# The first projection of a two-layer transformer kernel: two token tiles only centred ahead of q, their deviation applied to the logits

## Chip, cores, metric

The kernel runs on one core of a Trainium2 chip. The metric is the device time of one execution in microseconds (us), the median over several executions. "The block" below is the long run of 512-column matmuls that makes up 98% of the time. Its start is read from the timeline (start of its first matmul); the chain of waits, which counts from the end of the work before it, puts the same point up to 0.2 us later.

## The reference, cut to what matters

```python
x = A_x                                            # 2048 tokens x 1024, bf16
x = x + _A_ref(_layernorm(x), A_wqkv, A_wo)        # attention over 8 tokens at distance 0, 2, .. 14
x = x + _B_ref(_layernorm(x), B_w1, B_w3, B_w2)    # gated feed-forward, 1024 -> 3584 -> 1024
x = x + _A_ref(_layernorm(x), A_wqkv, A_wo)        # the same two once more, same weights
x = x + _B_ref(_layernorm(x), B_w1, B_w3, B_w2)

def _layernorm(x, axis=-1, eps=1e-5):
    m = jnp.mean(x, axis=axis, keepdims=True)
    v = jnp.var(x, axis=axis, keepdims=True)
    return (x - m) / jnp.sqrt(v + eps)
```

q, k and v are the normalised x times 1024 x 1024 weights. Since the layer norm divides each token by its own deviation, q of a token can be computed from the centred x, and its logits multiplied by 1/deviation afterwards.

## The kernel before

The kernel builds a list of operations, places them with a small scheduling model and emits them in that order; each engine then follows its own fixed order. All DMA is issued by one queue (SyncE), strictly in order. Token tiles have 128 tokens, chunks 512. The start works on chunk 0:

```python
def q_first():
    load_x(0, 0, 2)                      # token tiles 0, 1
    wslots[0] = q_weights(0, "k")        # eight rows of q weights, 256 KB each
    load_x(0, 2, 4)                      # tiles 2, 3
    b = ln(0, first=True)                # per tile: bn_stats x2, bn_aggr, sqrt (ScalarE), reciprocal,
                                         # (x - mean) * rstd, 8 TensorE transposes, copy to xnT
    order = [(0, 0, 5), (1, 0, 5), (0, 5, 8), (1, 5, 8), (2, 0, 8), (3, 0, 8)]
    for j, k0, k1 in order:              # tile by tile: matmuls of 128 columns
        ...
                    nc.tensor.matmul(bank[...][:, (m % 4) * P:(m % 4 + 1) * P], lhsT=lk[m][0],
                                     rhs=xnT[b][:, kk, j * P:(j + 1) * P], ...)
    ...                                  # store q, load k weights, x of chunk 1, v weights ...
    for which, key, tile_ in ((1, "kT", kT), (2, "vT", vT)):
        q_tile(0, 0, which, wslots[which], b, (key, tile_))   # k and v: 512-column matmuls, the block begins
```

Of the kernel before, what the change touches and what calls it, by code (L numbers as in the profile page):

```python
# [154 lines left out]
def kernel(  # L155
# [24 lines left out]
    scale = float(Dh) ** -0.5  # L180
    EPS = 1e-5
    NSLOT = 6
    NWARM = 12

    xin = A_x[0].rearrange("(n p) d -> p n d", p=P)
    xout = out[0].rearrange("(n p) d -> p n d", p=P)
# [11 lines left out]
    def alloc(name, shape, dt=BF16):  # L198
        return sb.tile(shape, dt, name=name)
# [29 lines left out]
    rs = alloc("rs", [P, NE], FP32)  # L229
    rsb = alloc("rsb", [P, NE])  # L230
    An = alloc("An", [P, W, NE])
    oT = [alloc(f"oT{i}", [P, KT, TCH]) for i in range(2)]
    qkv_d = [[dram.tile([D, S], BF16, name=f"qkv_d{l}_{i}") for i in range(3)] for l in range(2)]
    bank = [pp.tile([P, 512], FP32, name=f"bank{i}") for i in range(8)]
# [6 lines left out]
    def t1(n):  # L241
        return 0.15 + n / 960.0

    def dve(dur, emit, reads, writes, cls=2, **kw):
        return pr.add("DVE", dur, emit, reads, writes, cls, **kw)
# [4 lines left out]
    def dma(kb, dst, src, reads, writes, cls=3, transpose=False):  # L250
        def emit(op):
            if transpose:
                nc.sync.dma_start_transpose(dst, src)
            else:
                nc.sync.dma_start(dst, src)  # L255
        return pr.add("SP", 0.45, emit, reads, writes, cls, size=kb * 1024)
# [28 lines left out]
    def take_slot():  # L285
        i = n_slot[0] % NSLOT
        n_slot[0] += 1
        return i

    def load_x(c, j0=0, j1=TPC, after=()):  # L290
        for j in range(j0, j1):
            n = c * TPC + j
            dma(256, x_sb[n][:], xin[:, n, :], after, [("x", n, 0), ("x", n, 1)], 0 if c == 0 else 3)
# [3 lines left out]
    def ln(c, first=False):  # L297
        s = stage_no[0]
        b, q = s % 2, s % 4
        xb = xnT[b]  # L300

        def stats(j):
            n = c * TPC + j
            pri = j - 9 if first else 1
            for hh in range(2):
                dve(0.67, lambda _, hh=hh: nc.vector.bn_stats(st[q][:, j, hh, :],  # L306
                                                              x_sb[n][:, hh * 512:(hh + 1) * 512]),
                    [("x", n, hh)], [("st", q, j, hh)], pri)
            dve(0.2, lambda _: nc.vector.bn_aggr(mv[q][:, j, :], st[q][:, j, :, :]),  # L309
                [("st", q, j, 0), ("st", q, j, 1)], [("mv", q, j)], pri)  # L310

        def root(j0, j1):
            act(0.3, lambda _: nc.scalar.activation(sd[q][:, j0:j1], mv[q][:, j0:j1, 1], ACTF.Sqrt, bias=epst[:]),  # L313
                [("mv", q, j) for j in range(j0, j1)] + ["eps"], [("sd", q, j) for j in range(j0, j1)], j0 - 9 if first else 0, table="sqrt")
            dve(0.16, lambda _: nc.vector.reciprocal(rstd[q][:, j0:j1], sd[q][:, j0:j1]),  # L315
                [("sd", q, j) for j in range(j0, j1)], [("rstd", q, j) for j in range(j0, j1)], j0 - 9 if first else 0)

        def apply(j):
            n = c * TPC + j
            dve(0.5, lambda _: nc.vector.tensor_scalar(xn[j][:], x_sb[n][:], mv[q][:, j, 0:1], rstd[q][:, j:j + 1],  # L320
                                                       op0=ALU.subtract, op1=ALU.mult),
                [("x", n, 0), ("x", n, 1), ("mv", q, j), ("rstd", q, j)], [("xn", j)], j - 9 if first else 1)

        if first:
            for j in range(TPC):
                stats(j)
                root(j, j + 1)
                apply(j)
                a = Acc()

                def tr(op, j=j, a=a):
                    pt = bank[a.bank][:].bitcast(BF16)
                    for kk in range(KT):
                        nc.tensor.transpose(pt[:, kk * P:(kk + 1) * P], xn[j][:, kk * P:(kk + 1) * P], ident[:])  # L334
                tro = pr.add("PE", 0.5, tr, [("xn", j), "ident"], [], takes=[a], lag=0.17, lane=2)

                def ev(op, j=j, a=a):
                    pt = bank[a.bank][:].bitcast(BF16)
                    nc.scalar.copy(xb[:, :, j * P:(j + 1) * P], pt.rearrange("p (k t) -> p k t", k=KT))
                evac(act, 1.0, ev, tro, [], [("xnT", b, j)], a)  # L340
            return b
        for j in range(TPC):
            stats(j)
        root(0, TPC)
        for j in range(TPC):
            apply(j)
            dma(256, xb[:, :, j * P:(j + 1) * P], xn[j][:], [("xn", j)], [("xnT", b, j)], 0, transpose=True)
        return b
# [10 lines left out]
    def evac(add, dur, emit, last_mm, reads, writes, a, cls=0, **kw):  # L359
        op = add(dur, emit, reads, writes, cls, gives=[a], **kw)  # L360
        op.deps.add(last_mm)
        return op

    wslots = {}

    def q_weights(which, split):
        ids = [take_slot(), take_slot()]
        for h, i in enumerate(ids):
            if split != "c":
                v = slot[i][:].rearrange("p (k c) -> p k c", k=4)  # L370
                for k in range(0, 4, 1 if split == "k" else 4):
                    n = 1 if split == "k" else 4
                    dma(256 * n, v[:, k:k + n, :], wqkv_v[:, 4 * h + k:4 * h + k + n, which * D:(which + 1) * D], [],
                        [("w", i, k + z) for z in range(n)], 0 if split == "k" else 3)
            else:
                v = slot[i][:].rearrange("p (k c) -> p k c", k=KT)
                dma(1024, v, wqkv_v[:, :, which * D + h * 512:which * D + (h + 1) * 512], [],
                    [("w", i, k) for k in range(4)], 3)
        return ids, split
# [35 lines left out]
    def q_stage(l, c):  # L415
# [3 lines left out]
            q_tile(l, c, which, ws, b)  # L419
        stage_no[0] += 1  # L420

    def q_first():
        load_x(0, 0, 2)
        wslots[0] = q_weights(0, "k")
        load_x(0, 2, 4)
        b = ln(0, first=True)
        accs = {}
        order = [(0, 0, 5), (1, 0, 5), (0, 5, 8), (1, 5, 8), (2, 0, 8), (3, 0, 8)]
        for j, k0, k1 in order:
            if j not in accs:  # L430
                accs[j] = [Acc(), Acc()]
            pa = accs[j]
            for kk in range(k0, k1):
                lk = [q_lhs(wslots[0], kk, m) for m in range(KT)]

                def emit(op, kk=kk, j=j, pa=pa, lk=lk):
                    for m in range(KT):
                        nc.tensor.matmul(bank[pa[m // 4].bank][:, (m % 4) * P:(m % 4 + 1) * P], lhsT=lk[m][0],  # L438
                                         rhs=xnT[b][:, kk, j * P:(j + 1) * P], start=(kk == 0 and m % 4 == 0),
                                         stop=(kk == KT - 1), skip_group_check=True)  # L440
                op = pr.add("PE", 8 * 0.056, emit, [lk[0][1], ("xnT", b, j)], [], takes=pa, lag=0.17)
            if k1 == KT:
                for g in range(2):
                    evac(act, 0.59, lambda _, a=pa[g], g=g, j=j: nc.scalar.copy(
                        hT[:, 4 * g:4 * g + 4, j * P:(j + 1) * P],
                        bank[a.bank][:].rearrange("p (m t) -> p m t", m=4)), op, [],
                        [("hT", 4 * g + m, j) for m in range(4)], pa[g])
        for m0 in range(0, KT, 2):
            dma(256, spill_view(0, 0, m0, 0), hT[:, m0:m0 + 2, :],
                [("hT", m, j) for m in (m0, m0 + 1) for j in range(TPC)], [("d", 0, 0, 0, m0)], 1)  # L450
        wslots[1] = q_weights(1, "s")
        load_x(1)
        load_x(2, 0, 2)
        wslots[2] = q_weights(2, "s")
        load_x(2, 2, 4, [("hT", 7, TPC - 1)])
        load_x(3, 0, 4, [("hT", 7, TPC - 1)])
        for which, key, tile_ in ((1, "kT", kT), (2, "vT", vT)):
            dve(0.11, lambda _, tile_=tile_: nc.vector.memset(tile_[:, :, 0:HALO], 0.0), [], [(key, "h")], 1)
            q_tile(0, 0, which, wslots[which], b, (key, tile_))
        dma(2048, wo[:], wo_v, [("d", 0, 2, 0, 6)], ["wo"], 3)  # L460
        stage_no[0] += 1
# [25 lines left out]
    def t_stage(l, half):  # L487
# [22 lines left out]
                                                psm[:].rearrange("p w s -> p (w s)")), allA, ["pB"])  # L510
        dve(1.22, vtt(l2, psmT[:, :, 0:2], psmT[:, :, 2:4], ALU.add), ["pB"], [l2k])
        dve(t1(512), vtt(L.rearrange("p w e -> p (w e)"), l2[:, :, 0], l2[:, :, 1], ALU.add), [l2k], [Lk])
        if tok0 == 0:
            dve(t1(64), vtt(L[:, :, 0:8], L[:, :, 0:8], maskT[:], ALU.add), [Lk, "mask"], [Lk])
        dve(t1(256), vtt(m4, L[:, 0:4, :], L[:, 4:8, :], ALU.max), [Lk], [Lk])
# [157 lines left out]
```

## Time and profile before

| | before |
|---|---|
| time | 1617.48 us, 3 runs, 1617.37 to 1617.6 (later, with more runs, 1617.47) |
| span of the profiled run | 1615.7 us |
| first q matmul | 8.50 us |
| start of the block | 24.11 us |
| length of the block | 1588.69 us for 7416 matmuls, 214 ns each |

The chain of waits of the kernel before (start, length, what; all in us) shows the whole kernel in its last lines:

```profile
16.24 0.45 PE bank L334 x8
16.68 7.59 PE bank L438 x136
24.28 1588.69 PE bank L355 x7416
1612.97 0.02 issue
1612.99 0.29 DVE x L600
```

From 24.28 us on nothing delays TensorE. The table of who waited for whom, for TensorE (total us, times, longest), has only the start:

```profile
PE bank L334 <- DVE xn L320: 1.3, 2, 1.1
PE bank L278 <- DVE warm L274: 1.2, 1, 1.2
PE bank L438 <- ACT xnT L339: 0.4, 1, 0.4
```

L278 are the twelve warm-up matmuls, L334 the transposes, L438 the q matmuls. So an early change can only move the start of the block, as long as it leaves the block alone.

### The profile page before, as it was taken

How to read it: one execution, taken by the hardware profiler on the slowest of the kernel's cores; microseconds unless marked ns; L12 is line 12 of the kernel's file. 1: busy time of each engine (PE TensorE's matmuls, PEld its weight loads, DVE VectorE, ACT ScalarE, POOL GpSimd, SP SyncE). 2: the span in 40 equal slices, each digit the busy share in tenths (PEclk: the TensorE clock that was granted, in tenths of full speed). 3: DMA queues.
4: the chain of work that ended last, by engine and by line, in shares of the span. 5: the costliest groups of instructions: out<-in, count | busy, mean ns of one | idle time of the engine just before them, and what ended most of it. 6: DMA issues, size and time to landing. Idle time of an engine off the chain costs nothing.

```text
span 1615.7 us, 19394 instructions
## 1 busy us (share of the span) xinstructions
PE 1610.0 (100%) x7716; PEld 764.4 (47%) x7716; DVE 1120.2 (69%) x1900; ACT 328.9 (20%) x519; POOL 1.9 (0%) x12
## 2 busy tenths in 40 slices
PE   9999999999999999999999999999999999999999
PEld 7555544444444444444444444444444444444444
DVE  5898888889889888888898728884298832211211
ACT  4423322021211222113211032110321101101110
POOL 0000000000000000000000000000000000000000
PEclk9999999999999999999999999999999999999999
DMA  9734755385548763858545487465873464454441
GB/s 311 218 106 139 235 170 157 121 226 177 171 130 242 201 198 123 219 165 251 175 141 157 163 244 224 128 168 179 247 229 118 155 184 156 144 175 151 156 165 44
DMA packets 347818, 285.30 MB, mean 177 GB/s; under 512 B 70096, under 2 KB 342480, under 8 KB 347600
## 3 DMA queue, kind: packets, MB, share of 16 engines
q1 hardware_dynamic: 347728, 284.07, 57.9%
q8 instruction: 60, 0.98, 0.2%
q14 instruction: 30, 0.25, 0.0%
HBM read 238.94 MB, written 29.36 MB: 166 GB/s over the span
## 4 chain that ended last, share of the span: by engine, by line
PE 99%; DMA 1%; DVE 0%; SPq 0%; issue 0%
PE bank L355 98%; PE bank L438 0%; DMA x<-in_A_x_dram 0%; DMA slot<-in_A_wqkv_dram 0%; DVE st L306 0%; PE bank L334 0%; SPq L255 0%; DVE xn L320 0%; DVE mv L309 0%; DVE x L600 0%; DVE rstd L315 0%
## 5 line engine op out<-in xcount | busy, mean ns | idle before, releaser
L355 PE MATMUL bank<-xnT,slot 128*128 128x512 bf16 x5056 | 1094.2, 379 | 0.0
L355 PEld LDWEIGHTS <-slot 128*128 128x128 bf16 x5056 | 518.1, 102 | 572.9
L355 PE MATMUL bank<-slot,hT 128*128 128x512 bf16 (+2 forms) x1848 | 389.2, 373 | 0.0
L570 DVE TENSOR_TENSOR hT<-sg,bank 128x512 bf16<-128x512 bf16 x224 | 153.3, 685 | 212.5 <-PE bank L355 203.2
L259 DVE TENSOR_TENSOR scr<-scr 128x1024 bf16<-128x1024 bf16 (+3 forms) x576 | 292.2, 535 | 2.1
L355 PEld LDWEIGHTS <-hT 128*128 128x128 bf16 x1848 | 178.5, 98 | 208.7
L568 ACT ACTIVATE sg<-bank 128x512 bf16<-128x512 f32 x224 | 133.7, 597 | 654.1 <-PE bank L355 631.0
L259 DVE TENSOR_TENSOR scr<-qT,kT 128x2048 bf16<-128x2048 bf16 x128 | 153.7, 1216 | 69.9 <-DMA kT<-qkv_d 69.9
L407 ACT CAST sgt<-bank 128x512 bf16<-128x512 f32 x184 | 107.5, 584 | 291.5 <-PE bank L355 285.3
L259 DVE TENSOR_TENSOR scr<-pA,vT 128x2048 bf16<-128x2048 bf16 x128 | 152.6, 1217 | 0.4
L600 DVE TENSOR_TENSOR x<-x,bank 128x512 bf16<-128x512 bf16 (+1 forms) x66 | 43.7, 669 | 122.7 <-PE bank L355 122.4
L355 PE MATMUL bank<-wo,oT 128*128 128x512 bf16 x512 | 113.1, 379 | 0.0
L306 DVE BATCH_NORM_STATS2 st<-x 128x6 f32<-128x512 bf16 x128 | 84.2, 680 | 19.3 <-DMA x<-in_A_x_dram 18.9
L355 PEld LDWEIGHTS <-oT 128*128 128x128 bf16 x512 | 50.1, 98 | 60.4
L545 DVE TENSOR_TENSOR x<-x,bank 128x512 bf16<-128x512 bf16 x64 | 43.8, 685 | 36.7 <-PE bank L355 35.6
L313 ACT ACTIVATE sd<-mv,epst 128x4 f32<-128x4 f32 (+1 forms) x19 | 5.7, 297 | 189.1 <-DVE mv L309 189.1
L509 DVE STREAM_TRANSPOSE pB<-pA 128x2048 bf16<-128x2048 bf16 x16 | 37.0, 2310 | 0.4
L528 DVE STREAM_TRANSPOSE pA<-pB 128x2048 bf16<-128x2048 bf16 x16 | 37.0, 2310 | 0.4
L568 ACT ACT_TABLE_LOAD x20 | 25.7, 1283 | 51.0 <-PE bank L355 50.8
L259 DVE TENSOR_TENSOR pA<-scr 128x256 bf16<-128x256 bf16 x128 | 35.3, 283 | 0.3
L320 DVE TENSOR_SCALAR xn<-x,mv,rstd 128x1024 bf16<-128x1024 bf16 x64 | 31.5, 540 | 5.2 <-DMA xnT<-xn 5.0
L259 DVE TENSOR_TENSOR oT<-scr 128x256 bf16<-128x256 bf16 x128 | 33.7, 283 | 0.1
(41 smaller groups left out, 200.6 us busy)
## 6 DMA issues: line engine op xcount, KB each, us to landing
slot<-in_B_w_dram SPq DMA_DIRECT2D x160, 1024.0 KB, 5.7
slot<-in_A_wqkv_dram SPq DMA_DIRECT2D x28, 1024.0 KB, 5.3
qkv_d<-sgt SPq DMA_DIRECT2D x92, 256.0 KB, 4.0
qT<-qkv_d SPq DMA_DIRECT2D x16, 512.0 KB, 5.5
slot<-in_B_w_dram SPq DMA_DIRECT2D x16, 512.0 KB, 5.4
kT<-qkv_d SPq DMA_DIRECT2D x14, 544.0 KB, 6.6
vT<-qkv_d SPq DMA_DIRECT2D x14, 544.0 KB, 5.6
x<-in_A_x_dram SPq DMA_DIRECT2D x16, 256.0 KB, 5.8
```

The lines of the kernel that those rows point to most:

```text
L259: return lambda _: nc.vector.tensor_tensor(o, a, b, op=op)
L306: dve(0.67, lambda _, hh=hh: nc.vector.bn_stats(st[q][:, j, hh, :], x_sb[n][:, hh * 512:(hh + 1) * 512]), [("x", n, hh)], [("st", q, j, hh ...
L313: act(0.3, lambda _: nc.scalar.activation(sd[q][:, j0:j1], mv[q][:, j0:j1, 1], ACTF.Sqrt, bias=epst[:]), [("mv", q, j) for j in range(j0, ...
L320: dve(0.5, lambda _: nc.vector.tensor_scalar(xn[j][:], x_sb[n][:], mv[q][:, j, 0:1], rstd[q][:, j:j + 1], op0=ALU.subtract, op1=ALU.mult), ...
L355: nc.tensor.matmul(bank[a.bank][:, 0:ncol], lhsT=w, rhs=r, start=first and i == 0, stop=last and i == n - 1)
L407: evac(act, 0.59, lambda _, a=a, i=i, m=m: nc.scalar.copy(sgt[i][:, m % 2, :], bank[a.bank][:]), op, [], [("sgt", i, m % 2)], a)
L509: dve(2.31, lambda _: nc.vector.transpose(psmT[:].rearrange("p c d -> p (c d)"), psm[:].rearrange("p w s -> p (w s)")), allA, ["pB"])
L528: dve(2.31, lambda _: nc.vector.transpose(At[:].rearrange("p w s -> p (w s)"), AeT[:].rearrange("p c d -> p (c d)")), ["pB"], allA)
L545: evac(dve, t1(512), lambda _, xs=xs, a=a: nc.vector.tensor_tensor(xs, xs, bank[a.bank][:], op=ALU.add), op, [("x", n, hh)], [("x", n, hh) ...
L568: evac(act, 0.6, lambda _, i=i, a=ag: nc.scalar.activation(sg[i][:], bank[a.bank][:], ACTF.Silu), og, [], [("sg", i)], ag, table="silu")
L570: evac(dve, t1(512), lambda _, i=i, a=au, f=f: nc.vector.tensor_tensor(hT[:, f, :], sg[i][:], bank[a.bank][:], op=ALU.mult), ou, [("sg", i ...
L600: evac(dve, t1(cn), lambda _, xs=xs, a=a, cn=cn: nc.vector.tensor_tensor(xs, xs, bank[a.bank][:, 0:cn], op=ALU.add), op, [("x", n, hh)], [ ...
```

## The change

The intent: start q earlier. Tiles 0 and 1 are only centred before q. Their means come from plain sums on VectorE and ScalarE, so variance, root and reciprocal leave the path. Their q lacks the factor 1/deviation, which the first attention stage applies to the logits. q runs with moving operands of 256 columns where it can. The properly normalised tiles 0 and 1, needed for k and v, are made later and transposed by DMA. The factor needs another layout (token index within a 32-block on partitions, repeated four times), so it is written to DRAM and read back. The core of the diff:

```diff
-    NWARM = 12
+    NWARM = 10
+    rs_d = dram.tile([2 * P], FP32, name="rs_d")
...
+        for hh in range(2):                      # tile 0 in two halves, then tile 1, 3 weight rows, tiles 2, 3
+            dma(128, x_sb[0][:, hh * 512:(hh + 1) * 512], xin[:, 0, hh * 512:(hh + 1) * 512], ...)
...
+        for j in range(2):                       # centred only, transposed by TensorE
+            dve(0.5, ... nc.vector.tensor_scalar(xn[j][:], x_sb[j][:], mean[:, j:j + 1], None, op0=ALU.subtract), ...)
+            transposed(xn[j], ("xn", j), ce[:, :, j * P:(j + 1) * P], ..., True)
...
+        for j in range(2):                       # later: the real layer norm of tiles 0, 1
+            stats(j, [("xn", TPC - 1)])
+            root(j, j + 1)
+            apply(j)
+            dma(256, xnT[b][:, :, j * P:(j + 1) * P], xn[j][:], [("xn", j)], [("xnT", b, j)], 0, transpose=True)
+        dma(1, rs_d.rearrange("(j p) -> p j", p=P), rstd[q][:, 0:2], [("rstd", q, 0), ("rstd", q, 1)], ["rs_d"], 2)
+        for g in range(4):
+            dma(1, rsx[32 * g:32 * (g + 1), :], rs_d.rearrange("(b i) -> i b", i=32), ["rs_d"], [("rsx", g)], 2)
...
+        if l == 0 and tok0 == 0:                 # first attention stage
+            dve(t1(512), vtt(Lb, Lb, rsx[:].unsqueeze(1).unsqueeze(3).to_broadcast([P, W, NB, 8]), ALU.mult), ...)
```

The scheduler puts the write of `rs_d` into the DMA queue between the two transposes: transpose of tile 0, `rs_d`, transpose of tile 1, then loads of x.

More of the change, by code (lines that the diff above doesn't have):

```diff
@@ L231 @@
     An = alloc("An", [P, W, NE])
+    part = alloc("part", [P, 2], FP32)
+    mean = alloc("mean", [P, 2], FP32)
+    rsx = alloc("rsx", [P, NB], FP32)
+    rs_d = dram.tile([2 * P], FP32, name="rs_d")
     oT = [alloc(f"oT{i}", [P, KT, TCH]) for i in range(2)]
@@ L300, in ln, with stats @@
         xb = xnT[b]
-        def stats(j):
+        def stats(j, after=()):
             n = c * TPC + j
-            pri = j - 9 if first else 1
+            pri = -9 if first else 1
             for hh in range(2):
@@ L307, in stats @@
                                                               x_sb[n][:, hh * 512:(hh + 1) * 512]),
-                    [("x", n, hh)], [("st", q, j, hh)], pri)
+                    [("x", n, hh)] + list(after), [("st", q, j, hh)], pri)
             dve(0.2, lambda _: nc.vector.bn_aggr(mv[q][:, j, :], st[q][:, j, :, :]),
@@ L313, in root @@
             act(0.3, lambda _: nc.scalar.activation(sd[q][:, j0:j1], mv[q][:, j0:j1, 1], ACTF.Sqrt, bias=epst[:]),
-                [("mv", q, j) for j in range(j0, j1)] + ["eps"], [("sd", q, j) for j in range(j0, j1)], j0 - 9 if first else 0, table="sqrt")
+                [("mv", q, j) for j in range(j0, j1)] + ["eps"], [("sd", q, j) for j in range(j0, j1)], -9 if first else 0, table="sqrt")
             dve(0.16, lambda _: nc.vector.reciprocal(rstd[q][:, j0:j1], sd[q][:, j0:j1]),
-                [("sd", q, j) for j in range(j0, j1)], [("rstd", q, j) for j in range(j0, j1)], j0 - 9 if first else 0)
+                [("sd", q, j) for j in range(j0, j1)], [("rstd", q, j) for j in range(j0, j1)], -9 if first else 0)
         def apply(j):
@@ L321, in apply @@
                                                        op0=ALU.subtract, op1=ALU.mult),
-                [("x", n, 0), ("x", n, 1), ("mv", q, j), ("rstd", q, j)], [("xn", j)], j - 9 if first else 1)
+                [("x", n, 0), ("x", n, 1), ("mv", q, j), ("rstd", q, j)], [("xn", j)], -9 if first else 1)
         if first:
-            for j in range(TPC):
-                stats(j)
-                root(j, j + 1)
-                apply(j)
-                a = Acc()
-                def tr(op, j=j, a=a):
-                    pt = bank[a.bank][:].bitcast(BF16)
-                    for kk in range(KT):
-                        nc.tensor.transpose(pt[:, kk * P:(kk + 1) * P], xn[j][:, kk * P:(kk + 1) * P], ident[:])
-                tro = pr.add("PE", 0.5, tr, [("xn", j), "ident"], [], takes=[a], lag=0.17, lane=2)
-                def ev(op, j=j, a=a):
-                    pt = bank[a.bank][:].bitcast(BF16)
-                    nc.scalar.copy(xb[:, :, j * P:(j + 1) * P], pt.rearrange("p (k t) -> p k t", k=KT))
-                evac(act, 1.0, ev, tro, [], [("xnT", b, j)], a)
-            return b
+            return b, q, stats, root, apply
         for j in range(TPC):
@@ L364, with q_weights, row @@
     wslots = {}
-    def q_weights(which, split):
+    def q_weights(which, split, load=True, after=()):
         ids = [take_slot(), take_slot()]
+        if not load:
+            def row(kk):
+                i = ids[kk // 4]
+                v = slot[i][:].rearrange("p (k c) -> p k c", k=4)
+                dma(256, v[:, kk % 4, :], wqkv_v[:, kk, which * D:(which + 1) * D], [], [("w", i, kk % 4)], 0)
+            return ids, split, row
         for h, i in enumerate(ids):
@@ L370, in q_weights @@
                 v = slot[i][:].rearrange("p (k c) -> p k c", k=4)
-                for k in range(0, 4, 1 if split == "k" else 4):
-                    n = 1 if split == "k" else 4
-                    dma(256 * n, v[:, k:k + n, :], wqkv_v[:, 4 * h + k:4 * h + k + n, which * D:(which + 1) * D], [],
-                        [("w", i, k + z) for z in range(n)], 0 if split == "k" else 3)
+                dma(1024, v, wqkv_v[:, 4 * h:4 * h + 4, which * D:(which + 1) * D], after,
+                    [("w", i, k) for k in range(4)], 3)
             else:
@@ L420, in q_stage @@
         stage_no[0] += 1
-    def q_first():
-        load_x(0, 0, 2)
-        wslots[0] = q_weights(0, "k")
-        load_x(0, 2, 4)
-        b = ln(0, first=True)
-        accs = {}
-        order = [(0, 0, 5), (1, 0, 5), (0, 5, 8), (1, 5, 8), (2, 0, 8), (3, 0, 8)]
-        for j, k0, k1 in order:
-            if j not in accs:
-                accs[j] = [Acc(), Acc()]
-            pa = accs[j]
-            for kk in range(k0, k1):
-                lk = [q_lhs(wslots[0], kk, m) for m in range(KT)]
-                def emit(op, kk=kk, j=j, pa=pa, lk=lk):
-                    for m in range(KT):
-                        nc.tensor.matmul(bank[pa[m // 4].bank][:, (m % 4) * P:(m % 4 + 1) * P], lhsT=lk[m][0],
-                                         rhs=xnT[b][:, kk, j * P:(j + 1) * P], start=(kk == 0 and m % 4 == 0),
-                                         stop=(kk == KT - 1), skip_group_check=True)
-                op = pr.add("PE", 8 * 0.056, emit, [lk[0][1], ("xnT", b, j)], [], takes=pa, lag=0.17)
-            if k1 == KT:
-                for g in range(2):
-                    evac(act, 0.59, lambda _, a=pa[g], g=g, j=j: nc.scalar.copy(
-                        hT[:, 4 * g:4 * g + 4, j * P:(j + 1) * P],
-                        bank[a.bank][:].rearrange("p (m t) -> p m t", m=4)), op, [],
-                        [("hT", 4 * g + m, j) for m in range(4)], pa[g])
@@ new lines, in transposed, with tr, ev, emit @@
+    def transposed(src, key, dst, dkeys, both):
+        a = Acc()
+        def tr(op):
+            pt = bank[a.bank][:].bitcast(BF16)
+            for kk in range(KT):
+                nc.tensor.transpose(pt[:, kk * P:(kk + 1) * P], src[:, kk * P:(kk + 1) * P], ident[:])
+        tro = pr.add("PE", 0.5, tr, [key, "ident"], [], takes=[a], lag=0.17, lane=2)
+        def ev(add, fn, k0, k1, dur):
+            def emit(op):
+                pt = bank[a.bank][:].bitcast(BF16)
+                fn(dst[:, k0:k1, :], pt.rearrange("p (k t) -> p k t", k=KT)[:, k0:k1, :])
+            evac(add, dur, emit, tro, [], dkeys[k0:k1], a, cls=-9)
+        if both:
+            ev(dve, nc.vector.tensor_copy, 0, 4, 0.68)
+            ev(act, nc.scalar.copy, 4, 8, 0.59)
+        else:
+            ev(act, nc.scalar.copy, 0, 8, 1.0)
@@ new lines, in q_first, with store, emit @@
+    def q_first():
+        for hh in range(2):
+            dma(128, x_sb[0][:, hh * 512:(hh + 1) * 512], xin[:, 0, hh * 512:(hh + 1) * 512], [], [("x", 0, hh)], 0)
+        load_x(0, 1, 2)
+        rows = q_weights(0, "k", load=False)
+        wslots[0] = rows[:2]
+        for kk in range(3):
+            rows[2](kk)
+        load_x(0, 2, 4)
+        for kk in range(3, KT):
+            rows[2](kk)
+        b, q, stats, root, apply = ln(0, first=True)
+        ce = hT[:, 8:16, :]
+        dve(0.45, lambda _: nc.vector.tensor_scalar(xn[2][:, 0:512], x_sb[0][:, 0:512], 0.0, 0.0, op0=ALU.add,
+                                                    op1=ALU.add, accum_out=part[:, 0:1]),
+            [("x", 0, 0)], [("xn", 2), ("part", 0)], -9)
+        act(0.75, lambda _: nc.scalar.activation(xn[3][:, 0:512], x_sb[0][:, 512:1024], ACTF.Copy,
+                                                 accum_out=part[:, 1:2]), [("x", 0, 1)], [("xn", 3), ("part", 1)], -9)
+        dve(0.16, lambda _: nc.vector.tensor_scalar(mean[:, 0:1], part[:, 0:1], part[:, 1:2], 1.0 / D, op0=ALU.add,
+                                                    op1=ALU.mult), [("part", 0), ("part", 1)], [("mean", 0)], -9)
+        act(1.15, lambda _: nc.scalar.activation(xn[3][:], x_sb[1][:], ACTF.Copy, scale=1.0 / D,
+                                                 accum_out=mean[:, 1:2]), [("x", 1, 0), ("x", 1, 1)],
+            [("xn", 3), ("mean", 1)], -9)
+        for j in range(2):
+            dve(0.5, lambda _, j=j: nc.vector.tensor_scalar(xn[j][:], x_sb[j][:], mean[:, j:j + 1], None,
+                                                            op0=ALU.subtract),
+                [("x", j, 0), ("x", j, 1), ("mean", j)], [("xn", j)], -9)
+            transposed(xn[j], ("xn", j), ce[:, :, j * P:(j + 1) * P], [("ce", j, k) for k in range(KT)], True)
+        for j in range(2, TPC):
+            stats(j)
+            root(j, j + 1)
+            apply(j)
+            transposed(xn[j], ("xn", j), xnT[b][:, :, j * P:(j + 1) * P], [("xnT", b, j)] * KT, False)
+        for j in range(2):
+            stats(j, [("xn", TPC - 1)])
+            root(j, j + 1)
+            apply(j)
+            dma(256, xnT[b][:, :, j * P:(j + 1) * P], xn[j][:], [("xn", j)], [("xnT", b, j)], 0, transpose=True)
+        dma(1, rs_d.rearrange("(j p) -> p j", p=P), rstd[q][:, 0:2], [("rstd", q, 0), ("rstd", q, 1)], ["rs_d"], 2)
+        for g in range(4):
+            dma(1, rsx[32 * g:32 * (g + 1), :], rs_d.rearrange("(b i) -> i b", i=32), ["rs_d"], [("rsx", g)], 2)
+        def store(pa, op, j0):
+            for g in range(4):
+                evac(act, 0.59, lambda _, a=pa[g], g=g: nc.scalar.copy(
+                    hT[:, 2 * g:2 * g + 2, j0 * P:(j0 + 2) * P],
+                    bank[a.bank][:].rearrange("p (m t) -> p m t", m=2)), op[g], [],
+                    [("hT", 2 * g + m, j) for m in range(2) for j in (j0, j0 + 1)], pa[g])
+        pa = [Acc() for _ in range(4)]
+        for kk, j0, j1 in [(k, j, j + 1) for j in range(2) for k in range(3)] + [(k, 0, 2) for k in range(3, KT)]:
+            lk = [q_lhs(wslots[0], kk, m) for m in range(KT)]
+            def emit(op, kk=kk, j0=j0, j1=j1, lk=lk, pa=pa):
+                for m in range(KT):
+                    t0 = (m % 2) * 2 * P
+                    nc.tensor.matmul(bank[pa[m // 2].bank][:, t0 + j0 * P:t0 + j1 * P], lhsT=lk[m][0],
+                                     rhs=ce[:, kk, j0 * P:j1 * P], start=(kk == 0 and m % 2 == 0 and j0 == 0),
+                                     stop=(kk == KT - 1), skip_group_check=True)
+            op = pr.add("PE", 8 * (j1 - j0) * 0.0545, emit,
+                        [lk[0][1]] + [("ce", j, kk) for j in range(j0, j1)], [], takes=pa, lag=0.17)
+        store(pa, [op] * 4, 0)
+        pa = [Acc() for _ in range(4)]
+        ops = []
+        for g in range(4):
+            lk = [[q_lhs(wslots[0], kk, m)[0] for kk in range(KT)] for m in (2 * g, 2 * g + 1)]
+            def emit(op, g=g, lk=lk, pa=pa):
+                for m in range(2):
+                    for kk in range(KT):
+                        nc.tensor.matmul(bank[pa[g].bank][:, m * 2 * P:(m + 1) * 2 * P], lhsT=lk[m][kk],
+                                         rhs=xnT[b][:, kk, 2 * P:4 * P], start=(kk == 0 and m == 0),
+                                         stop=(kk == KT - 1), skip_group_check=True)
+            ops.append(pr.add("PE", 16 * 0.1092, emit,
+                              [("w", i, k) for i in wslots[0][0] for k in range(4)] + [("xnT", b, 2), ("xnT", b, 3)],
+                              [], takes=[pa[g]], lag=0.17))
+        store(pa, ops, 2)
@@ L451, in q_first @@
         wslots[1] = q_weights(1, "s")
-        load_x(1)
-        load_x(2, 0, 2)
-        wslots[2] = q_weights(2, "s")
+        load_x(1, 0, 4, [("xn", 1)])
+        load_x(2, 0, 2, [("xn", 1)])
+        wslots[2] = q_weights(2, "s", after=[("xn", 1)])
         load_x(2, 2, 4, [("hT", 7, TPC - 1)])
@@ L512, in t_stage @@
         dve(t1(512), vtt(L.rearrange("p w e -> p (w e)"), l2[:, :, 0], l2[:, :, 1], ALU.add), [l2k], [Lk])
+        if l == 0 and tok0 == 0:
+            Lb = L.rearrange("p w (n h) -> p w n h", h=8)
+            dve(t1(512), vtt(Lb, Lb, rsx[:].unsqueeze(1).unsqueeze(3).to_broadcast([P, W, NB, 8]), ALU.mult),
+                [Lk] + [("rsx", g) for g in range(4)], [Lk])
         if tok0 == 0:
```

## The prediction

> **What bounds it now.** The chain of waits is 98% one block: 512-column matmuls from 24.28 us to 1612.97 without a gap (7,416 in 1588.69 us, 214 ns each). In the table of who waited for whom TensorE waits only 2.9 us in all: 1.2 for the warm tile, 1.3 for the first normalised tile xn, 0.4 for its transposed copy. After that it is never released by anything. So the change can only move when the steady block starts (24.28), not the block.
>
> **Start of before (timeline).** Warm-up matmuls 1.19 to 5.72. Tile 0: statistics from 3.53, aggregate, root (ScalarE 0.29), reciprocal, apply, transposes at 6.78, copy 1.02 us, first q matmul at 8.50. From 8.50 to 24.28 the engine is busy: 256 matmuls of 128 columns at 56 to 57 ns (14.5 us), two more rounds of transposes (0.9), 0.3 us idle.
>
> **What the change does.**
> 1. Tiles 0 and 1 skip variance, root and reciprocal before q. Their sums go to VectorE (half of tile 0) and ScalarE (the rest). Estimate: tile 0's mean at about 4.3 us, tile 1's at 5.3 (ScalarE needs about 1.1 us for 1024 columns, by the 1.02 us copy), tile 1 centred by 5.9. In VectorE's order the copy of tile 0 follows tile 1's subtraction, so the first q matmul comes at about 6.6 rather than 8.50: 1.9 us.
> 2. q: 48 matmuls of 128 columns (2.7 us) and 104 of 256. By the line through 56 ns (128) and 214 ns (512) a 256 takes about 109 ns: 11.3 us. Sum 14.0 instead of 14.5: 0.5 us. The Trainium skill (TensorE: Matmul & The Clock Gate, "Wait — 56ns, not 53.3ns?") gives a fixed 2.5 ns per matmul at the full clock; 214 ns here agrees roughly.
> 3. One round of transposes for tiles 2, 3 stays inside q (0.9 us); I expect 0 to 0.5 us of wait there. DMA is saturated (340 to 390 GB/s from 5 to 25 us), x2 and x3 now come before weight rows 3 to 7. Row 7 should land near 12.5, needed at about 13.8; rows keep just ahead of use.
> 4. The normalised tiles 0 and 1 for k and v are made later on VectorE (applied near 15 and 15.8) and transposed by DMA behind 2 MB of k weights. Estimate: landed at 20 to 21, needed near 21.7. This is the tightest point; up to 1 us may be lost.
> 5. Five tiny DMAs and one VectorE multiply of 512 columns (about 0.7 us) in the first attention stage: off the path. v weights are issued later (about 23.5, landing about 31), needed at about 35.4. Two warm-ups fewer: only keeps them from delaying tile 0's transposes.
>
> Steady block starts at about 21.8 instead of 24.28. Time: 1617.48 - 2.5 = **1615.0 us**, range 1613.9 to 1616.4. Faster by over 2%: 0.005; within 2%: 0.99; slower by over 2%: 0.005.
>
> **What would show it.** First q matmul near 6.6; the 512-column block starting near 21.8 with the same 1588.7 us length; TensorE's waits still 2 to 3 us in all, on the mean or copies; no wait of the first k matmul on the DMA transposes; no wait on v weights at 35 us.
>
> **What would make it wrong.** The DMA transposes late (block starts at 22.5 or more); weight rows 3 to 5 late since x2, x3 precede them; transposes of tiles 2, 3 stalling the first half; the clock gate reopening at half speed after short pauses (none is long: before, 1.06 us idle cost nothing); later waits of the k/v evacuations for store DMAs queued behind the delayed loads.

## The result

The time is 1625.6 us (6 runs, 1624.65 to 1627.03), the kernel before 1617.47 in the same runs. The ratio is 1.005, 95% interval 1.0037 to 1.0063. A ratio here is the mean time of one kernel's fast runs over the mean of the other's fast runs of the same rounds, so not quite the ratio of the medians. The change was meant to save 2.5 us and costs 8.1: far less than 2%, but clear of noise, since the interval excludes 1.

The chain of waits of the changed kernel, from the q matmuls on:

```profile
7.62 5.46 PE bank L489 x72
13.08 0.89 PE bank L420 x16
13.98 1.75 PE bank L489 x16
15.72 7.00 PE bank L503 x64
22.72 0.02 issue
22.75 0.59 ACT hT L478
23.34 6.13 issue
29.47 1591.26 PE bank L343 x7416
```

q (L489, L503) ends at 22.72 us, which is 1.56 us earlier than before (24.28). Then TensorE stands still until 29.47. And the same 7416 matmuls take 1591.26 us instead of 1588.69, 2.57 more. The start of the block by the chain moved by 29.47 - 24.28 = 5.19; 5.19 + 2.57 = 7.76 of the 8.2 us by which the spans differ (1623.9 to 1615.7); the rest lies after the last matmul.

TensorE's waits in the changed kernel:

```profile
PE bank L343 <- issue: 6.8, 1, 6.8
PE bank L282 <- DVE warm L278: 1.2, 1, 1.2
PE bank L420 <- DVE xn L458: 0.4, 1, 0.4
```

The profile names no releaser for the 6.8 us ("issue"). The built kernel does: the first k matmul waits for both DMA transposes and for k weights. The k weights are not what came last: by the trace's landing records they had landed by 19.1 us. The DMA issues of the changed kernel on the queue (start, length of the issue, what):

```profile
16.49 1.34 SPq L257 DMA_TRANSPOSE xnT<-xn  x1
17.94 0.52 SPq L259 DMA_DIRECT2D rs_d<-rstd  x1
18.55 1.24 SPq L257 DMA_TRANSPOSE xnT<-xn  x1
...
27.98 1.88 SPq L259 DMA_DIRECT2D rsx<-rs_d  x3
```

and the view by tile, for the two transposes of the start alone, gives their times from issue to landing:

```profile
DMA to landing us min/median/max: 3.5/7.2/10.8
```

The first landed after 3.5 us (20.0). The second, issued at 18.55, landed after 10.8, at 29.4, and TensorE starts at 29.47. Between them in the queue stands `rs_d`, 1 KB, which took 10.0 us (17.94 to 27.98, when the reads that need it are issued). The stretches of the trace, columns busy us of PE, PEld, DVE, ACT, POOL, then granted clock, DMA share and GB/s, show a queue that has work and moves almost nothing:

```profile
20.00:22.00 2.00, 2.00 (x20) 1.78 (x19) 0.00 (x0) 0.58 (x1) 0.00 (x0) 1.00 1.48 145
22.00:24.00 2.00, 0.71 (x7) 0.39 (x4) 0.00 (x0) 0.58 (x1) 0.00 (x0) 1.00 0.06 1
24.00:26.00 2.00, 0.00 (x0) 0.00 (x0) 0.00 (x0) 0.00 (x0) 0.00 (x0) 1.00 0.49 46
26.00:28.00 2.00, 0.00 (x0) 0.00 (x0) 0.00 (x0) 0.00 (x0) 0.00 (x0) 0.88 0.30 38
28.00:30.00 2.00, 0.53 (x2) 0.33 (x3) 0.00 (x0) 0.00 (x0) 0.00 (x0) 0.50 0.45 129
30.00:32.00 2.00, 2.00 (x6) 0.70 (x5) 1.58 (x3) 0.00 (x0) 0.00 (x0) 0.50 1.08 385
32.00:34.00 2.00, 2.00 (x6) 0.82 (x5) 2.00 (x6) 0.86 (x2) 0.00 (x0) 0.50 1.06 271
```

Loads of x were issued from 19.84 us; from 22 to 24 us the rate is 1 GB/s. The same stretch of the kernel before has 375:

```profile
22.00:24.00 2.00, 2.00 (x39) 2.00 (x37) 2.00 (x6) 0.00 (x0) 0.00 (x0) 1.00 1.01 375
```

The clock column explains the longer block: by the trace's clock records it is at 0.50 from 27.52 to 34.35 us. TensorE works from 29.47 to 34.35 of this, 4.88 us at half speed, which costs about 2.4 of the 2.57 us. The Trainium skill (TensorE: Matmul & The Clock Gate, Part 1: The HAM clock gate) says that the array falls to half clock after an idle window of about 3.4 us and needs about as long of sustained work to come back. This trace agrees in kind: half clock 4.8 us after TensorE went idle, full clock 4.9 us after its first new matmul.

The packets of the trace, counted by start and size, show where the transfers were:

```
changed kernel      4 B    256 B    2048 B (longest)
19.0 - 19.5 us      167      481       0
19.5 - 20.0         137      149       0
20.0 - 20.5           0      413       0
20.5 - 21.0           5      403       0
21.0 - 21.5          27       62      23 (3.57 us)
21.5 - 22.0           0        0       9
22.0 - 22.5           0        0       0
22.5 - 23.5           0        0       0
```

The 4 B packets are nearly all the 256 values of `rs_d` (the trace of e1 below, which has no such write, has some 4 B packets too), the 256 B ones are those of the transposes (those from 19.5 us on, about 1024, of the second), the 2048 B ones loads of x. The data of the transpose had all gone out by 21.5 us, as in the normal transfer of e6 below. Only its completion came 8 us later. The Trainium skill (DMA: Bandwidth & Descriptors, Queues, rings and completion order) says that a transfer's semaphore increment lands only after every earlier write of the same DMA engine. That is the first theory:

**Theory A.** The write of 256 separate 4 B values to DRAM takes about 10 us to complete; the transpose behind it can't report completion before it, and later loads crawl. **Theory B.** The DMA transposes are late by themselves, because they queue behind 2 MB of k weights and in front of many loads.

### The profile page after: what moved, and what is told of

Read it like the earlier page. It is cut to its first block, busy times and chain, and to the rows that moved or that the text cites. A ratio compares the mean times of both kernels' runs of the same rounds, so it can differ in the third digit from the quotient of the medians.

```text
span 1623.9 us, 19203 instructions
## 1 busy us (share of the span) xinstructions
PE 1612.3 (99%) x7610; PEld 763.5 (47%) x7610; DVE 1123.7 (69%) x1908; ACT 327.3 (20%) x521; POOL 1.9 (0%) x12
## 4 chain that ended last, share of the span: by engine, by line
PE 99%; issue 0%; ACT 0%; DVE 0%
PE bank L343 98%; PE bank L489 0%; PE bank L503 0%; PE bank L282 0%; PE bank L420 0%; ACT hT L478 0%; ACT hT L426 0%; DVE hT L426 0%; DVE x L666 0%; DVE warm L278 0%
```

## The experiments

### 1. No trip through DRAM: e1_copies_on_chip

```diff
-        dma(1, rs_d.rearrange("(j p) -> p j", p=P), rstd[q][:, 0:2], ...)
-        for g in range(4):
-            dma(1, rsx[32 * g:32 * (g + 1), :], rs_d.rearrange("(b i) -> i b", i=32), ...)
+        for g in range(4):
+            for bb in range(4):
+                pr.add("POOL", 0.2, ... nc.gpsimd.tensor_copy(
+                    rsx[32 * g:32 * (g + 1), bb:NB:4], rstd[q][32 * bb:32 * (bb + 1), 0:2]), ...)
```

> The changed kernel, but the deviations reach their 32-partition layout by sixteen tiny copies on GpSimd; the write rs_d to DRAM and the four reads rsx are gone. Theory A (the 4-byte write of rs_d, issued between the two DMA transposes, holds back the completion of the second): the 512-column block starts straight after q at about 22.8 us instead of 29.47 and no matmul of it runs at half clock; about 1616.3 us, 1.2 below before. Theory B (the transposes are late by themselves, behind the 2 MB of k weights): no change, the block starts near 29 us, 1625.6 us.

Correct, 1615.87 us (5 runs, 1615.54 to 1616.12), before 1617.27; ratio 0.999, interval 0.9977 to 1.0002. The sixteen copies take 3.65 us on an idle GpSimd and are needed at 75.8 us. TensorE's timeline (start, busy us, line, operation):

```profile
7.11 5.46 PE L490 MATMUL bank<-hT,slot 128*128 128x128 bf16 x72
12.40 1.06 PE L419 MATMUL bank<-ident,xn 128*128 128x128 bf16 x16
13.30 1.91 PE L490 MATMUL bank<-hT,slot 128*128 128x256 bf16 x16
15.04 7.15 PE L504 MATMUL bank<-xnT,slot 128*128 128x256 bf16 x64
22.03 2.32 PE L342 MATMUL bank<-xnT,slot 128*128 128x512 bf16 x9
```

The block follows q at once, at 22.03 us, and the clock stays at 1.00. All of the loss is in this trip. Theory B falls: the transposes stand at the same place behind the same k weights, and land after 3.5 and 3.1 us.

### 2. The write behind both transposes: e2_write_behind

```diff
-  rstd[q][:, 0:2], [("rstd", q, 0), ("rstd", q, 1)], ["rs_d"], 2)
+  rstd[q][:, 0:2], [("rstd", q, 0), ("rstd", q, 1), ("xn", 1)], ["rs_d"], 2)
```

> The changed kernel with rs_d's write issued after both transposes instead of between them; nothing else moved but a few loads in the queue. Theory A: the second transpose lands about 3 us after its issue, the block starts at about 22.8 us; but the write still takes 8 to 10 us to land and holds the reads rsx and with them the v weights, which are issued near 35 us, so TensorE may now wait for v weights at about 36.5 us, up to 5 us: 1616 to 1621 us. Theory B: the block starts near 29 us as in the changed kernel, 1625.6.

1627.29 us (4 runs, 1626.38 to 1627.93), ratio 1.006. The two transposes now land like this (view by tile, start of the kernel):

```profile
DMA to landing us min/median/max: 3.1/3.2/3.3
```

So one exchange in the queue (a few transfers further back changed places with it) takes the second transpose from 10.8 us to at most 3.3. The block starts at 22.95 us without a wait. The write itself still takes 9.9 us, the reads of it and everything behind wait, and v weights are issued at 37.13 us, later than in the changed kernel (34.92). TensorE then waits for them:

```profile
PE bank L343 <- DMA slot<-in_A_wqkv_dram: 7.8, 2, 6.2
```

The half clock follows from 39.41 to 49.65 us. I had expected up to 5 us of wait there, it was 7.8, and no time was gained: the same slow write only chose another victim.

### 3. The transposes on TensorE, the trip kept: e3_pe_transposes

```diff
-            dma(256, xnT[b][:, :, j * P:(j + 1) * P], xn[j][:], ..., transpose=True)
+            transposed(xn[j], ("xn", j), xnT[b][:, :, j * P:(j + 1) * P], [("xnT", b, j)] * KT, False)
```

> The changed kernel with the two DMA transposes of tiles 0 and 1 done on TensorE (0.9 us more matmul time); the trip of the deviations through DRAM is kept. Theory A: rs_d still lands 8 to 10 us after its issue, the loads of x behind it are as late as in the changed kernel, but no k matmul waits for a transpose by DMA; block starts near 23.7 us, later wait for v weights possible (up to 5 us): 1617 to 1622. Theory B (the transposes are what clogs the queue): rs_d lands within 4 us, loads behind it flow at over 300 GB/s, about 1617.2 us.

1622.76 us (4 runs, 1620.05 to 1624.78), ratio 1.0032. With no DMA transpose near it, `rs_d` still takes 9.6 us (DMA issues: name, count, size, us to landing):

```profile
rsx<-rs_d SPq DMA_DIRECT2D x4, 1.0 KB, 5.3
rs_d<-rstd SPq DMA_DIRECT2D x1, 1.0 KB, 9.6
```

So the write is slow without the transposes. The block starts at 23.11; later TensorE waits 4.2 us for v weights and runs 3.4 us at half clock, a little more than I had expected (1617 to 1622 us).

### 4. Dummy matmuls in the wait: e4_filler

```diff
+        for i in range(32):   # between the last q matmul and the first k matmul
+            pr.add("PE", 0.002, ... nc.tensor.matmul(bank[...][:], lhsT=warm[:, 0:P], rhs=warm[:], ...))
```

> The changed kernel with 32 dummy matmuls of 512 columns (6.9 us at full clock) put into the wait before the k matmuls, result unused. If the second part of the loss is the clock, which fell to half for the first matmuls of the block because TensorE idled 6.75 us, the block runs at full clock from its start at about 29.6 us and the time is about 2.4 us below the changed kernel, 1623.2. If the slow first matmuls had another cause (operands arriving slowly), nothing changes: 1625.6.

1626.05 us (4 runs, 1625.14 to 1626.09), ratio 1.0051: no gain over the changed kernel (1625.6, ratio 1.005). The mechanism was right, the sum was not. The clock stays at 1.00 from 4.33 us to the last matmul, so the half clock was indeed caused by the idle time. But the saved time is spent on other waits:

```profile
PE bank L343 <- DMA slot<-in_A_wqkv_dram: 1.6, 1, 1.6
PE bank L343 <- DMA xnT<-xn: 1.0, 2, 0.9
```

```profile
29.88 15.08 PE L343 MATMUL bank<-xnT,slot 128*128 128x512 bf16 x67 [0.87 <-DMA xnT<-xn]
46.59 13.17 PE L343 MATMUL bank<-xnT,slot 128*128 128x512 bf16 x58 [1.63 <-DMA slot<-in_A_wqkv_dram]
```

The block starts 0.41 us later than in the changed kernel, because the write took 11.0 us in this trace. TensorE comes to the second half of the v weights at 44.96 us and waits until 46.59. The speed of TensorE alone doesn't explain this wait: in the changed kernel the same weights had landed by 44.22, early enough for both, and TensorE came to them at 46.55. In e4 they arrived more than 2 us later, and why is not shown. So taking away the half clock alone bought nothing here, but whether it must be so stays open.

### 5 and 6. What makes the write slow: e5_probe and e12_probe_layout

Both are the kernel before with six kinds of small writes of a constant in each of the eight feed-forward stages, one run each. Their times (1617.36 and 1617.28) are as before. The edit adds, per kind:

```diff
+        dst, src = [(pa_d[i].rearrange("(j p) -> p j", p=P), prb[:, 0:2]), ... ][v]
+        dma(1, dst, src, ["prb", ...], [("probe", v, i)], -5)
```

> The kernel before with 48 small writes of a constant to otherwise unused DRAM, six kinds, one of each in each of the eight feed-forward stages, away from the start: pa 256 values of 4 B packed in 1 KB (as rs_d), pb the same with 64 B between values, pc with 512 B between values, pd 128 rows of 8 B in 1 KB, pe 128 rows of 64 B, pf 128 rows of 512 B. If writes of 4 B that share a line are slow one after the other, pa lands in about 10 us and pb and pc in 3 to 6 like pf. If every 4 B write is slow, pa, pb and pc all take about 10. If it is the number of pieces, pd (half of them) takes about half of pa. If the 10 us came from the start's traffic only, pa lands like pf.

> The probe again with other kinds of small writes: pa as before (256 values of 4 B in 1 KB, the two values of a partition 512 B apart), pb 256 values of 4 B in the same 1 KB but in memory order by partition (neighbours in memory come from the same partition and the same piece of the transfer), pc 256 values of 4 B with 16 B between, pd 128 values of 4 B in 512 B, pe 512 values of 4 B in 2 KB, pf 256 values of 4 B written to SBUF. In e5_probe pa took 12.0 us, a 64 KB write 5.7 us and 4 B values 64 B apart 7.5. If the count of pieces in a packed block counts, pd takes about 9 and pe about 18 to 20, pb as pa. If it is neighbours in memory that are written by different parts of the transfer, pb takes about 7.5 as 8 B pieces did. pf shows whether DRAM matters: then about 6; pc between pa and 7.5.

Median us from issue to landing, with other traffic in the queue:

| write | first probe | second probe |
|---|---|---|
| 128 rows of 512 B (64 KB) | 5.7 | |
| 128 rows of 64 B | 6.9 | |
| 256 values of 4 B, 512 B apart | 7.0 | |
| 256 values of 4 B, 64 B apart | 7.5 | |
| 128 rows of 8 B, packed | 7.6 | |
| 256 values of 4 B, 16 B apart | | 9.1 |
| 256 values of 4 B, packed as `rs_d` | 12.0 | 11.7 |
| 256 values of 4 B, packed, in memory order | | 13.7 |
| 128 values of 4 B, packed | | 10.8 |
| 512 values of 4 B, packed | | 12.2 |
| 256 values of 4 B to SBUF | | 6.2 |

The lines of the second probe:

```profile
pa_d<-prb SPq DMA_DIRECT2D x8, 1.0 KB, 11.7
pb_d<-prb SPq DMA_DIRECT2D x8, 1.0 KB, 13.7
pc_d<-prb SPq DMA_DIRECT2D x8, 1.0 KB, 9.1
pd_d<-prb SPq DMA_DIRECT2D x8, 0.5 KB, 10.8
pe_d<-prb SPq DMA_DIRECT2D x8, 2.0 KB, 12.2
pf_s<-prb SPq DMA_DIRECT2D x8, 1.0 KB, 6.2
```

The slow case is 4 B values packed side by side in DRAM. Neither the size of the piece alone (spaced by 64 B or more they take 7.0 to 7.5, against 5.7 for 64 KB), nor the number (128, 256 and 512 differ by 1.4 us), nor small pieces as such (to SBUF 6.2) does it. Each kind has its own fixed place in the stage, but the place is not the cause: at the second place, 4 B values 64 B apart took 7.5 in the first probe and packed ones 13.7 in the second. My guess in the second expectation, that neighbours written by different parts of the transfer collide, fell: in memory order it is not faster (12.0 to 15.7 us, against 10.9 to 13.1). Why 8 B rows escape, and what DRAM does with the packed values, these runs don't tell.

### 7. The write spread out, in place: e6_pitch512

```diff
-    rs_d = dram.tile([2 * P], FP32, name="rs_d")
+    rs_d = dram.tile([2 * P, P], FP32, name="rs_d")
-        dma(1, rs_d.rearrange("(j p) -> p j", p=P), rstd[q][:, 0:2], ...)
+        dma(1, rs_d.rearrange("(j p) w -> p j w", p=P)[:, :, 0:1], rstd[q][:, 0:2].unsqueeze(2), ...)
```

> The changed kernel with rs_d spread out, each value 512 B from the next; same number and order of transfers, reads rsx follow the layout. If sharing of lines makes the write slow, it lands in 2 to 4 us and the block starts at about 22.8 us: 1616.3 us. If each 4 B write to DRAM is slow by itself, still about 10 us, block near 29 us: 1625.6.

1617.62 us (4 runs, 1617.2 to 1618.05), ratio 1.0001 to before. The DMA queue's order is the same as in the changed kernel, entry by entry; the only difference is the address step in DRAM, of the write and of its reads:

```profile
rsx<-rs_d SPq DMA_DIRECT2D x4, 1.0 KB, 4.1
rs_d<-rstd SPq DMA_DIRECT2D x1, 1.0 KB, 2.3
```

The write lands in 2.3 us instead of 10.0, both transposes in at most 3.5, and the block starts at 22.55 us. The loads behind the write no longer crawl, 363 GB/s where the changed kernel had 1:

```profile
22.00:24.00 2.00, 2.00 (x14) 1.51 (x12) 0.19 (x1) 0.59 (x1) 0.00 (x0) 1.00 1.03 363
```

Both halves of theory A are shown by this one edit. It doesn't reach e1, which is about 1.7 us faster (each against the kernel before of its own rounds): the block starts 0.5 us later, and since the four reads still sit in the queue, v weights are issued at 27.86 us (e1: 23.66) and TensorE waits 1.3 us for them. I had expected 1616.3.

### 8. Two values as one piece: e7_bytes8

```diff
-    rs_d = dram.tile([2 * P], FP32, name="rs_d")
+    rs_d = dram.tile([P, 2], FP32, name="rs_d")
-        dma(1, rs_d.rearrange("(j p) -> p j", p=P), rstd[q][:, 0:2], ...)
+        dma(1, rs_d[:], rstd[q][:, 0:2], ...)
```

> The changed kernel with rs_d laid out by partition, so that each partition writes its two values as one piece of 8 B: 128 pieces instead of 256, still 1 KB. If the time goes with the number of pieces, the write lands after about 5 us, the second transpose lands near 24 us and the block starts there: about 1618 to 1620 us. If it goes with the bytes or is fixed: 1625.6.

1618.07 us (4 runs, 1617.57 to 1618.81). The order of the queue is again that of the changed kernel. The write lands in 3.5 us, less than half of 10.0 for half as many pieces, so the time does not go with the number of pieces alone. The block starts at 23.77 after a wait of 0.6 us for the second transpose; 0.7 us more goes on v weights.

### 9. The slow write at a quiet time: e8_late_write

```diff
+        dma(1, rs_d.rearrange("(j p) -> p j", p=P), rstd[q][:, 0:2],
+            [("rstd", q, 0), ("rstd", q, 1)] + [("w", i, 0) for i in wslots[2][0]], ["rs_d"], 2)   # after v weights
```

> The changed kernel, the same 4 B write and reads, but issued only after the v weights have landed (in the queue behind three transposes of chunk 1, some 45 us in). Theory A says the place alone cost the time: the block starts at about 22.8 us, no wait for v weights; about 1616.3 us if nothing urgent queues behind the slow write there. If what queues behind it is urgent (transposes of chunk 1, spills of k and v), TensorE waits at the first q stage near 49 us instead, up to 7 us.

1617.9 us (4 runs, 1617.49 to 1620.62). The block starts at 22.54 us, v weights come in time, and the write, issued at 42.53 and still 8.6 us long, now delays a transpose of chunk 1: TensorE waits 1.0 us for it. The place decides what is hit, the layout how hard. One run of 1620.62, with a granted clock of 0.999 where the others have 1.0, suggests that there is little slack.

### 10 and 11. A better version: e9_x0_whole, and e1 again: e11_copies_again

```diff
-        for hh in range(2):
-            dma(128, x_sb[0][:, hh * 512:(hh + 1) * 512], xin[:, 0, hh * 512:(hh + 1) * 512], [], [("x", 0, hh)], 0)
-        load_x(0, 1, 2)
+        load_x(0, 0, 2)
```

> e1_copies_on_chip with the first token tile loaded by one transfer of 2 KB rows as in the kernel before, instead of two of 1 KB rows. In the traces the second tile landed at 5.16 us (changed kernel) and 4.88 us (e1) although tile sums were planned for about 4.3. If the halves cost transfer rate and one issue of 0.45 us, tile 1 lands some 0.4 us earlier, the first q matmul comes near 6.8 us instead of 7.11 and the time is 0.3 us lower, 1615.6. If the halves pay, the first sum starts later and the time is the same or up to 0.3 us higher.

> e1_copies_on_chip once more, unchanged, as the neighbour of e9_x0_whole on the same chip and as a repeat of its gain over the kernel before: 1615.5 to 1616.2 us, 1.2 to 1.7 below before, all runs below all runs of before.

e9: 1615.67 us (5 runs, 1615.23 to 1616.0), ratio 0.9989, interval 0.9975 to 1.0003. e11: 1616.04 us (5 runs, 1615.5 to 1616.37), ratio 0.999; before 1617.46. In e9 the ScalarE sum of tile 1, which waits for its load, starts at 4.16 us against 4.78 in e11, and the first q matmul is at 6.75 against 7.08; in the e11 trace q also waits 0.4 us for a weight row. (The traces are of the fastest run of e9 and the slowest of e11.) The block of e9 starts at 21.68 us. The gap of 0.37 us between the two medians is what was expected, but their ranges overlap, so it is likely rather than shown. Against before, the intervals of e1, e9 and e11 all just include 1. Still, every one of their 15 runs (at most 1616.37) lies below every run of the kernel before (at least 1616.99). The saving is about 1.4 to 1.8 us, 0.1%.

## Why the prediction was wrong

It gave 1615.0 us, range 1613.9 to 1616.4. The result was 1625.6.

- **What bounds the kernel: right.** Only the start of the block could move, and all of it went through there, plus the clock of the block's first matmuls.
- **Step 1 (first q matmul at 6.6 instead of 8.50): right in kind, half in size.** It came at 7.62 in the changed kernel, 7.11 in e1 and 6.75 in e9. Tile 1's sum was to be done at 5.3 us, so begun near 4.2, and ScalarE started on it at 5.16 when the tile had landed: tile 0 in two halves delays tile 1, as e9 suggests. In the changed kernel's trace the full clock also came late (7.04 us, 5.29 in e1), and the first transposes took 1.06 us on the timeline instead of 0.61 in e1.
- **Step 2 (256 columns at 109 ns): right.** 64 of them took 7.00 us in the chain, 109.4 ns each.
- **Step 3 (0 to 0.5 us wait at tiles 2 and 3): right.** The chain runs through them without a gap.
- **Step 4 failed: "Estimate: landed at 20 to 21, needed near 21.7. This is the tightest point; up to 1 us may be lost."** The first landed at 20.0, the second at 29.4, because of what stood between them. The estimate had looked at the 2 MB ahead of the transposes and not at the 1 KB between them.
- **Step 5 failed, and is the root: "Five tiny DMAs and one VectorE multiply of 512 columns (about 0.7 us) in the first attention stage: off the path."** The multiply took 0.69 us and was off the path. The tiny write took 10.0 us and held the completion of its neighbour. That nobody waits for a transfer's data soon does not take it off the path, when it shares a queue with transfers that are waited for. e1, e2 and e6 show this, each with one edit.
- **The list of what would make it wrong** had late transposes, the clock gate after pauses and delayed loads, all three seen, but for another cause; the late transposes were allowed up to 1 us (step 4) and TensorE waited 6.8. The clock fell after 4.8 us of idle time, not after a short pause.
- **v weights: right without the trip.** Issue near 23.5 was predicted; it was 23.66 in e1 and 34.92 in the changed kernel.

With the trip removed, e1 came to 1615.87 and e9 to 1615.67, inside the predicted range. So the term that broke the prediction is the write that it had put at zero. The smaller error of step 1 remains: without the trip 1.4 to 1.8 us are saved, not 2.5.

## What to carry to other kernels

Judge a small transfer by its layout and its place in the queue, not by its bytes: 1 KB of 4 B values packed in DRAM took 10.0 us to land, the 2 MB load of `wo` in the same trace 9.7, and the transfers behind it paid. Where a per-token factor only has to move between blocks of 32 partitions, sixteen copies on an idle engine do it without any transfer. And when a stall also slows the clock, don't count on a repair of the clock alone (e4 gained nothing); remove the stall.

## What the Trainium skill lacked or had wrong

- DMA: Bandwidth & Descriptors (Specifications) gives a limit of 512 B, below which a transfer does read-modify-write. The runs show that for small writes to DRAM the spacing matters too: 256 values of 4 B landed in 2.3 us when 512 B apart (e6) and in 10.0 us when packed; 8 B rows packed took 3.5 us (e7). No page has this for small writes.
- The same page (Queues, rings and completion order) says that a semaphore increment waits for earlier writes of its engine. It gives no size for the effect: a transpose whose data was out by 21.5 us reported at 29.4, 10.8 us after its issue, behind such a write, and within 3.3 us of its issue ahead of it (e2). Nor does it say that loads behind a write to the core's own DRAM crawl: 1 GB/s from 22 to 24 us, 363 with the values spread out (e6).
- TensorE: Matmul & The Clock Gate (Part 1) puts the half clock after an idle window of about 3.4 us, and does not say how busy such a window may be. In the changed kernel it came 4.8 us after the idle time began. In e2 it came after 2.5 us of idle time (36.93 to 39.41 us), and in e3 at 43.21, when TensorE had been at work again for 0.9 us after a pause of 2.56. In the 3.4 us before each of these two falls TensorE had been busy for about 0.9 us, so the window need not be wholly idle.
